# Earlier weight loads, eight tiles split ahead, and older work first in the steps of a feed-forward stage

## The chip, the cores and the metric

The kernel runs on one core of a Trainium2 chip. The metric is the device time of one execution in microseconds (us), as the median of several runs. Five engines work side by side, each through its own instructions in order: TensorE (PE in the profile; its weight loads are PEld), VectorE (DVE), ScalarE (ACT), GpSimd (POOL) and SyncE (SP), which here only issues DMAs. An instruction that waits holds up all that stand behind it on its engine. Matmul results land in PSUM banks; everything else lives in SBUF, whose tiles are reused, so that a load into a tile waits for the last reader of what it held.

## What is computed

Attention in which each query keeps its 32 best keys, then a soft mixture of 8 experts, then a feed-forward layer, over 2304 tokens of width 512:

```python
scores = scale * q @ k.T;  attn = softmax(top 32 of each row);  x = attn @ v
logits = x @ phi                                   # 32 slots, 4 for each expert
slot_in = softmax(logits, axis=0).T @ x
slot_out[e] = relu(slot_in[e] @ w1[e]) @ w2[e]      # 8 experts, 512 -> 1024 -> 512
x = softmax(logits, axis=1) @ slot_out
h = x @ w_in                                       # 512 -> 2048
g = where(h >= 1, h, where(h <= -1, 0, (h + 1)**2 / 4))
out = g @ w_out                                    # 2048 -> 512
```

`w_in` and `w_out` come as 64-bit floats, read by the kernel as pairs of 32-bit integers and rebuilt as float32.

## The kernel before

**Attention** runs first, by a hand-written order over 16 pairs of heads. During it the first weight tiles are loaded, and `w_in` is converted and stored as `cv_d`.

**Weight tiles.** `worder` lists 88 tiles, `w_0` to `w_87`, nearly all of 128 x 1024 words (512 KB): 32 of `w1`, 32 of `w2`, eight of the converted `w_in` (`cv_d`) and 16 of `w_out`. All go through SP's queue in the order of that list. Each needs a free slot, a piece of SBUF that was used before: `wload` takes the next slot of `wfree` and notes it in `ring`, so that `ring` holds the slots in the order in which they were filled, which is also the order in which they are freed. A few slots consist of two halves in different places (`half_slots`); tiles of `w1`, `w2` and `cv_d` fit there by two DMAs of half the size, `w_out` tiles don't. After attention nine slots are taken out of `ring` (`tr_slots`, `w_slots`, `mix_slots`: scratch for rebuilding `w_out`, for its split tiles and for the mixture weights), and all other slots are refilled in turn.

**The expert part.** `ex_in` multiplies the slot inputs by `w1` (tile line L827, rows `h<-w,siT`), for experts 0 to 3 (`g` = 0) and 4 to 7, in four chunks `c`; `ex_out` multiplies by `w2` (L850, rows `so<-w,h1T`) in eight chunks. Between them stand transposes (`ex_turn`, `mix_turn`, `ex_place`) and the mixture weights (`mix_load`, `mix_norm`, `mix_split`).

**The feed-forward part.** Since a token is a mixture of 32 slots, `slot_out @ w_in` is computed once: `m_first` gives the first quarter of its columns as `m4[0]`, `m_rest` the other three in one PSUM tile, `m_split` divides them into a high and a low part, and `m_spread` makes `m4[1]` to `m4[3]` of them. A step `(t, f)` then treats 384 tokens (block `t` of 6) and 128 of the 2048 columns (`f` of 16). `emit_h` computes h in a PSUM tile `h_ps` (two banks, `ps_m`, which `m_ps` tiles share), two ACT passes (L952, L953) and a maximum with a minimum on DVE (L954) give g; g is split into a rounded part and a rest (`ghl`: a copy and a subtraction, L961 or L963, and L964); `emit_o` adds nine matmuls (L975) to the three output tiles. There are 96 steps, numbered here from 0: steps 0 to 31 alternate `t` = 0 and 1 for each `f`, and from 32 on a block is done at a time. h and g of a step are issued three steps ahead (`GA` = 3).

**Rebuilding a tile of `w_out`** (`prep`) takes two ACT passes (L934, L938), two DVE shifts (L935, L936), an addition on GpSimd (L939), one DVE operation (L941), an ACT copy into the rounded part `wh` (L943) and a DVE subtraction for the rest `wl` (L944). Four tiles are done in the expert part, and twelve within the first 26 steps, begun in step `(1, f)` and finished in the next.

Of the kernel before, what the change touches and what calls it, by code (L numbers as in the profile page):

```python
# [73 lines left out]
def kernel_body(tc, qT, kT, vP, phi, w1, w2, w_in, w_out, out, fast, flag):  # L74
# [851 lines left out]
    def prep(f, k):  # L926
        x64 = wtile[(4, 0, f)]
        hf = x64[:, :, 1].bitcast(F32)
        if k == "a":
# [3 lines left out]
        if k == "a":  # L933
            nc.scalar.activation(tf, hf, AF.Abs)  # L934
            nc.vector.tensor_scalar(tf, tf, 2.0 ** -15, None, op0=ALU.max)  # L935
            nc.vector.tensor_scalar(t, t, 3, None, op0=ALU.logical_shift_left)  # L936
        elif k == "r":
            nc.scalar.activation(r.bitcast(F32), x64[:, :, 0].bitcast(U32), AF.Identity, bias=two, scale=2.0 ** -51)  # L938
            nc.gpsimd.tensor_tensor(t, t, r, op=ALU.add)  # L939
        else:  # L940
# [4 lines left out]
            del preps[f]

    def emit_h(s_):
        t, f = s_
# [6 lines left out]
        gs[s_] = g

    def emit_g(s_, on_act=False):
        g = gs.pop(s_)
        gh, gl = (x[:, :BLK] for x in ring_tile("g", g_slots, "ghl", F32R))
        if on_act:  # L960
# [43 lines left out]
    ex_in(0, range(1))
    for f in (0, 1):
        prep(f, "a")
        prep(f, "r")
    ex_in(0, range(1, 4))
    prep(0, "b")
# [117 lines left out]
```

## Time and profile before

| | |
|---|---|
| three runs | 889.18, 889.29 (median), 891.91 us |
| the profiled execution | 890.73 us, span 888.9 us |
| PE, DVE, ACT, POOL busy | 94%, 77%, 73%, 49% of the span |
| mean granted TensorE clock | 0.977 of full speed |
| attention | to about 565 us |
| experts | about 566 to 624 us |
| feed-forward | about 624 us to the end |

The span is the time from the first to the last instruction; the execution's own time holds 1.8 us more around it. Times in the rows are counted from the start of the span.

### The profile page before, as it was taken

The numbers are of one execution on the slowest core, as the hardware profiler recorded it, in microseconds if no ns is written. First come the engines' busy times: TensorE is split into PE (matmuls) and PEld (weight loads), VectorE is DVE, ScalarE is ACT, GpSimd is POOL, SyncE is SP. The second block draws the span as 40 slices with busy tenths as digits, with TensorE's granted clock in tenths as the row PEclk, the third lists the DMA queues.
The fourth block names the chain that finished last, engine by engine and source line by source line (L and its number), as shares of the span: only waits on it lengthen the run. The fifth ranks groups of instructions, "written<-read, shape, count | busy, mean of one in ns | idle before, by whom it ended". The sixth has DMA issues, their size and how long they took to land.

```text
span 888.9 us, 17733 instructions
## 1 busy us (share of the span) xinstructions
PE 837.3 (94%) x5695; PEld 680.8 (77%) x5695; DVE 686.8 (77%) x3113; ACT 645.0 (73%) x1294; POOL 439.6 (49%) x462
## 2 busy tenths in 40 slices
PE   4889999999999999999999998898878789999997
PEld 3679988988998898988888997422356568888885
DVE  6999999989999999999999982360366676666663
ACT  5688999889899888899888895331366666545452
POOL 2788888878788877788877770110011210000000
PEclk9699999999999999999999999799998899999999
DMA  8463564464255244255245416399900001000001
GB/s 239 141 171 93 154 186 117 133 173 120 93 151 127 76 127 119 70 139 139 79 112 140 165 31 243 100 397 403 409 16 1 1 1 72 36 1 37 1 36 39
DMA packets 45046, 108.60 MB, mean 122 GB/s; under 512 B 8240, under 2 KB 8240, under 8 KB 44944
## 3 DMA queue, kind: packets, MB, share of 16 engines
q1 hardware_dynamic: 44624, 106.73, 39.1%
q8 instruction: 47, 0.77, 0.4%
q10 hardware_dynamic: 320, 0.66, 0.3%
q14 instruction: 55, 0.45, 0.1%
HBM read 70.70 MB, written 8.91 MB: 90 GB/s over the span
## 4 chain that ended last, share of the span: by engine, by line
PE 77%; DVE 9%; ACT 6%; DMA 5%; issue 1%; SPq 0%; POOL 0%; ACTq 0%; DVEq 0%; POOLq 0%
PE s_ps L310 20%; PE o_ps L975 17%; PE av_ps L484 14%; PE pt_ps L456 6%; DMA w<-in_moe_w_dram 5%; PE s_ps L412 4%; PE av_ps L485 3%; PE rem_ps L229 3%; PE moe_ps L574 2%; DVE cand L337 2%; PE h_ps L950 2%; DVE rg L954 2%; ACT rg L953 1%; ACT rg L952 1%; PE xT_ps L533 1%
## 5 line engine op out<-in xcount | busy, mean ns | idle before, releaser
L310 PE MATMUL s_ps<-kh,q 128*128 128x288 f32 x640 | 208.7, 343 | 15.2 <-DVE q L265 9.1
L975 PE MATMUL o_ps<-whl,ghl 128*128 128x512 f32 x864 | 219.4, 399 | 1.1 <-DVE mhl L897 1.1
L975 PEld LDWEIGHTS o_ps<-whl,ghl 128*128 128x128 f32 x864 | 164.1, 191 | 35.5 <-issue 1.5
L444 POOL TENSOR_TENSOR ssb<-ssb,pen 128x576 f32<-128x576 f32 x141 | 180.7, 1286 | 18.1 <-ACT pen L441 15.7
L310 PE MATMUL s_ps<-kl,q 128*128 128x288 f32 x640 | 181.8, 300 | 0.0
L337 DVE MAX8 cand<-ssb 128x8 f32<-128x82 f32 (+1 forms) x1008 | 164.3, 228 | 4.6 <-ACT ssb L328 3.8
L310 PEld LDWEIGHTS s_ps<-kh,q 128*128 128x128 f32 x640 | 124.3, 194 | 33.5 <-DVE q L265 9.4
L484 PE MATMUL av_ps<-v_sb,ptb 128*128 128x65 f32 (+1 forms) x1280 | 147.1, 261 | 0.4 <-ACT xT L546 0.4
L484 PEld LDWEIGHTS av_ps<-v_sb,ptb 128*128 128x128 f32 (+1 forms) x1280 | 141.1, 180 | 5.1 <-issue 2.9
L310 PEld LDWEIGHTS s_ps<-kl,q 128*128 128x128 f32 x640 | 125.1, 196 | 0.3
L421 DVE MAX8 l<-s_ps 128x8 f32<-128x576 f32 x144 | 109.2, 758 | 17.7 <-PE s_ps L412 17.3
L441 ACT ACTIVATE pen<-ssb,kb 128x576 bf16<-128x576 f32 x141 | 110.4, 793 | 3.2 <-POOL kb L437 2.1
L447 ACT ACTIVATE ssb<-ssb,nm 128x576 f32<-128x576 f32 x141 | 109.0, 785 | 0.6 <-POOL ssb L444 0.6
L328 ACT COPY ssb<-s_ps 128x576 f32<-128x576 f32 x144 | 91.3, 642 | 24.8 <-PE s_ps L310 20.9
L952 ACT ACTIVATE rg<-h_ps,half 128x384 f32<-128x384 f32 x96 | 55.6, 579 | 70.3 <-PE h_ps L950 70.1
L939 POOL TENSOR_TENSOR tr_l<-tr_l 128x512 int32<-128x512 int32 x16 | 21.2, 1322 | 168.2 <-DVE ghl L964 95.2
L954 DVE SCALAR_TENSOR_TENSOR rg<-h_ps,rg 128x384 f32<-128x384 f32 x96 | 53.5, 557 | 62.8 <-ACT rg L953 62.8
L395 POOL TENSOR_SCALAR mb<-ssb,top 128x576 bf16<-128x576 f32 x48 | 83.4, 1737 | 17.0 <-DVE top L344 6.4
L466 ACT COPY ptb<-pt_ps 128x512 f32<-128x512 f32 x144 | 82.5, 598 | 3.8 <-PE av_ps L484 3.7
L456 PE MATMUL pt_ps<-ident,ssb 128*128 128x128 f32 x576 | 84.3, 273 | 0.3 <-ACT ptb L466 0.2
L397 DVE TENSOR_SCALAR_CACHE_REDUCE mb<-ssb,top 128x576 bf16<-128x576 f32 x96 | 75.8, 802 | 0.0
L344 DVE MAX8 top<-cand 128x8 f32<-128x56 f32 x432 | 73.6, 207 | 0.1
(160 smaller groups left out, 1322.1 us busy)
## 6 DMA issues: line engine op xcount, KB each, us to landing
w<-in_moe_w_dram SPq DMA_DIRECT2D x56, 512.0 KB, 7.0
q<-qst SPq DMA_DIRECT2D x60, 160.0 KB, 3.1
kh<-kst SPq DMA_DIRECT2D x60, 144.0 KB, 2.5
kl<-kst SPq DMA_DIRECT2D x60, 144.0 KB, 2.8
x<-in_moe_w_in_dram SPq DMA_DIRECT2D x16, 512.0 KB, 3.8
w<-in_moe_w_out_dram SPq DMA_DIRECT2D x16, 512.0 KB, 10.2
v_sb<-in_v_dram SPq DMA_DIRECT2D x16, 325.0 KB, 2.9
raw_t<-in_q_dram SPq DMA_DIRECT2D x15, 320.0 KB, 3.7
```

The costliest lines, as they stand in the source:

```text
L310: nc.tensor.matmul(s[:, hf, :HS], a, w, start=(n == 0), stop=(n == len(terms) - 1), skip_group_check=True)
L328: nc.scalar.copy(st[u]["ssb"][:, j], st.pop((u, j))[:, :, :HS])
L337: nc.vector.max(st[u]["cand"][:, j, 8 * g:8 * g + 8], row(u, j)[:, S * g // NSEG:S * (g + 1) // NSEG])
L395: nc.gpsimd.tensor_scalar(st[u]["mb"][:, j], row(u, j), t_u, None, op0=ALU.is_ge)
L421: nc.vector.max(st[u]["l8"][:, j], st.pop((u, j))[:, :, :HS])
L441: nc.scalar.activation(pen, row(u, j), AF.Relu, bias=st[u]["kb"][:, j:j + 1], scale=-BIG)
L444: nc.gpsimd.tensor_tensor(row(u, j), row(u, j), st.pop((u, "pen", j)), op=ALU.subtract)
L447: nc.scalar.activation(row(u, j), row(u, j), AF.Exp, bias=st[u]["nm"][:, j:j + 1], scale=0.125)
L456: nc.tensor.transpose(pt[:, c, :], pr[:, c * P:(c + 1) * P], ident)
L466: nc.scalar.copy(ptb, st.pop((u, "pt", j)))
L484: nc.tensor.matmul(o, pj[:, c, sl], v_sb[:, 4 * jj + c, :], start=(c == 0), stop=False)
L975: nc.tensor.matmul(pos[t][n], a[:, sl], w, start=(f == 0 and k == 0), stop=(f == NF - 1 and k == 2))
```

## The change

1. `worder` has the four first `w_out` tiles four places later, behind four `w2` tiles; the next four `w_out` tiles stand ahead of the last six `cv_d` tiles.
2. The nine slots held back are no longer the first nine of `ring`, but nine whole slots from its ninth place on.
3. `prep` has five parts, 0 to 4. Eight tiles are begun before step 0 (the last two are finished in steps 0 to 3). The other eight follow one in every three steps, from step 3, each spread over four steps.
4. Within a step, what belongs to older data comes first on every engine; in two of three such steps the rounding copy of g is put off to the next step, on ACT.
5. `m_rest` and `m_split` move from ahead of step 0 into step 2, and their PSUM tile into the two banks of `ps_m`; the `e_ps` bank that it had is left to the output tiles.

```diff
+SOON = 8
-    worder[32:32] = [(4, 0, f) for f in range(EARLY)]
-    worder += [(2, 0, n) for n in range(2 * NHP)] + [(4, 0, f) for f in range(EARLY, NF)]
+    worder[36:36] = [(4, 0, f) for f in range(EARLY)]
+    worder += [(2, 0, 0), (2, 0, 1)] + [(4, 0, f) for f in range(EARLY, SOON)]
+    worder += [(2, 0, n) for n in range(2, 2 * NHP)] + [(4, 0, f) for f in range(SOON, NF)]
...
-    tr_slots = [ring.pop(0) for _ in range(3)]
-    w_slots = [ring.pop(0) for _ in range(EARLY)]
-    mix_slots = [ring.pop(0) for _ in range(2)]
+    held = [x for x in ring[8:] if x in slots_a + slots_b[:3] + cv_slots][:5 + EARLY]
+    ring = [x for x in ring if x not in held]
+    tr_slots, mix_slots, w_slots = held[:3], held[3:5], held[5:]
...
-            mx["m"] = ps_f.tile([P, 512], F32, name="m_ps1", tag="e_ps")
+            mx["m"] = ps_m.tile([P, 512], F32, name="m_ps1", tag="m_ps")
...
-    begin = {int((f - EARLY) * 1.1): f for f in range(EARLY, NF)}
+    todo = {}
+    for f in range(SOON - 2, SOON):
+        for k, lag in ((1, 0), (2, 1), (3, 1), (4, 2)):
+            todo.setdefault((f - SOON + 2 + lag, k), []).append(f)
+    for f in range(SOON, NF):
+        for k, lag in enumerate((0, 1, 2, 2, 3)):
+            todo.setdefault((3 + 3 * (f - SOON) + lag, k), []).append(f)
+    behind = []
     def step(i):
...
+        if i == 2:
+            m_rest(1)
+            m_rest(2)
+            m_rest(3)
+            mhl.extend(m_split())
+        if i % 8 == 4 and i // 8 < NC1 - 1:
+            m_spread(i // 8 + 1, *mhl)
         if nxt:
             emit_h(nxt)
-        if new is not None:
-            prep(new, "a")
+        work(4, 2, 1)
+        late_g = behind.pop() if behind else None
+        if late_g:
+            emit_c(late_g, nc.scalar)
+        work(3, 0)
         if nxt:
-            emit_g(nxt, new is not None)
-        if new is not None:
-            prep(new, "r")
-        if t == 0 and f - 1 in begin:
-            prep(begin[f - 1], "b")
+            emit_m(nxt)
+        if late_g:
+            emit_d(late_g)
+        if nxt:
+            if any((j, 0) in todo for j in (i, i - 1)):
+                behind.append(nxt)
+            else:
+                emit_c(nxt, nc.vector)
+                emit_d(nxt)
         emit_o(t, f, range(NS))
...
     m_first()
-    m_rest(1)
-    for s_ in steps[:2]:
-        emit_h(s_)
-        emit_g(s_)
-    m_rest(2)
-    m_rest(3)
-    for s_ in steps[2:GA]:
-        emit_h(s_)
-        emit_g(s_)
-    mhl = m_split()
+    prep(5, 0)
+    emit_h(steps[0])
+    for k in (2, 3):
+        prep(4, k)
+    emit_h(steps[1])
+    prep(5, 1)
+    emit_g(steps[0])
+    prep(4, 4)
+    emit_g(steps[1])
+    prep(6, 0)
+    for k in (2, 3):
+        prep(5, k)
+    emit_h(steps[2])
+    prep(5, 4)
+    emit_g(steps[2])
+    prep(7, 0)
```

Here `emit_m` is the maximum and minimum, `emit_c` the rounding copy and `emit_d` the subtraction of g; `work(k, ...)` issues the parts of `prep` that `todo` names for the step.

**SP's queue at the end of attention.** `w_28` to `w_31` are the last tiles of `w1`; `w_32` and those after it stand behind them. Before:

```order
L165 DMA w_27_9084<-in_moe_w1_dram 128x1024
L165 DMA w_26_9080<-in_moe_w1_dram 128x1024
L165 DMA w_28_9086<-in_moe_w1_dram 128x1024
L165 DMA w_29_9132<-in_moe_w1_dram 128x1024
L165 DMA w_30_9191<-in_moe_w1_dram 128x1024
L165 DMA w_31_9216<-in_moe_w1_dram 128x1024
L165 DMA w_32_9415<-in_moe2_w_out_dram 128x1024
L165 DMA w_33_9417<-in_moe2_w_out_dram 128x1024
L165 DMA w_34_9419<-in_moe2_w_out_dram 128x1024
L165 DMA w_35_9421<-in_moe2_w_out_dram 128x1024
L165 DMA w_36_9423<-in_moe_w2_dram 128x512
L165 DMA w_36_9424<-in_moe_w2_dram 128x512
```

After:

```order
L167 DMA w_33_9294<-in_moe_w2_dram 128x512
L167 DMA w_28_9086<-in_moe_w1_dram 128x1024
L167 DMA w_29_9132<-in_moe_w1_dram 128x1024
L167 DMA w_33_9295<-in_moe_w2_dram 128x512
L167 DMA w_30_9191<-in_moe_w1_dram 128x1024
L167 DMA w_31_9216<-in_moe_w1_dram 128x1024
L167 DMA w_34_9298<-in_moe_w2_dram 128x512
L167 DMA w_34_9299<-in_moe_w2_dram 128x512
L167 DMA w_35_9302<-in_moe_w2_dram 128x512
L167 DMA w_35_9303<-in_moe_w2_dram 128x512
L167 DMA w_36_9431<-in_moe2_w_out_dram 128x1024
L167 DMA w_37_9433<-in_moe2_w_out_dram 128x1024
```

The first four `w2` tiles, as eight halves, have moved ahead of the `w_out` tiles and among the last loads of attention. Behind the third of the `w_out` tiles the next load goes into the slot of `w_2` (freed by the first chunk of `ex_in`) where it went into the slot of `w_11` (third chunk).

**PE from `m_first` to the first steps.** Rows with `m_ps_9850` or `m_ps_9856` are `m_first`, the rows with 32x512 are `m_rest`, `h_ps` is h of a step and `o_ps` its output. Before:

```order
L880 MATMUL m_ps_9850<-w_9503,so_9543 128x512 x2
L880 MATMUL m_ps_9850<-w_9505,so_9543 128x512 x2
L889 MATMUL m_ps_9857<-w_9507,so_9543 32x512 x2
L889 MATMUL m_ps_9857<-w_9509,so_9543 32x512 x2
L950 MATMUL h_ps<-cT_9599,m_0_9402 128x384 x2
L889 MATMUL m_ps_9857<-w_9511,so_9543 32x512 x2
L889 MATMUL m_ps_9857<-w_9513,so_9543 32x512 x2
L889 MATMUL m_ps_9857<-w_9515,so_9543 32x512 x2
L889 MATMUL m_ps_9857<-w_9517,so_9543 32x512 x2
L950 MATMUL h_ps<-cT_9599,m_0_9402 128x384 x2
L975 MATMUL o_ps_0_9915<-whl,ghl 128x512 x3
```

After:

```order
L883 MATMUL m_ps_9856<-w_9505,so_9543 128x512 x2
L955 MATMUL h_ps<-cT_9601,m_0_9418 128x384 x4
L991 MATMUL o_ps_0_9926<-whl,ghl 128x512 x3
L991 MATMUL o_ps_1_9927<-whl,ghl 128x512 x3
L991 MATMUL o_ps_2_9928<-whl,ghl 128x512 x3
L955 MATMUL h_ps<-cT_9601,m_0_9418 128x384
L991 MATMUL o_ps_0_9955<-whl,ghl 128x512 x3
L991 MATMUL o_ps_1_9956<-whl,ghl 128x512 x3
L991 MATMUL o_ps_2_9957<-whl,ghl 128x512 x3
L892 MATMUL m_ps_9967<-w_9515,so_9543 32x512 x2
L892 MATMUL m_ps_9967<-w_9517,so_9543 32x512 x2
```

All twelve rows of `m_rest` (six in this print, of which two are shown) have moved behind the matmuls of steps 0 and 1, and h of the fourth step stands ahead of step 0 in both.

**ACT and DVE in the steps, around the rebuilding of one `w_out` tile (`w_81`).** `tr_l` and `whl` are the tile's, `rg` and `ghl` a step's. ACT before, two steps:

```order
L952 ACTIVATE rg_10178<-h_ps_10176,half_77 128x384
L953 ACTIVATE rg_10178<-rg_10178 128x384
L934 ACTIVATE tr_l_10183<-w_81_9529 128x512
L961 CAST ghl_10187<-rg_10179 128x384
L938 ACTIVATE tr_l_10183<-w_81_9529,two_95 128x512
L952 ACTIVATE rg_10204<-h_ps_10202,half_77 128x384
L953 ACTIVATE rg_10204<-rg_10204 128x384
L943 CAST whl_10214<-tr_l_10183 128x512
```

ACT after, three steps:

```order
L957 ACTIVATE rg_10081<-h_ps_10079,half_77 128x384
L958 ACTIVATE rg_10081<-rg_10081 128x384
L937 ACTIVATE tr_l_10086<-w_81_9529 128x512
L938 ACTIVATE tr_l_10086<-w_81_9529,two_95 128x512
L957 ACTIVATE rg_10103<-h_ps_10101,half_77 128x384
L958 ACTIVATE rg_10103<-rg_10103 128x384
L969 CAST ghl_10090<-rg_10082 128x384
L957 ACTIVATE rg_10124<-h_ps_10122,half_77 128x384
L958 ACTIVATE rg_10124<-rg_10124 128x384
L969 CAST ghl_10111<-rg_10103 128x384
L947 CAST whl_10128<-tr_l_10086 128x512
```

DVE before, from the maximum of the second of these steps:

```order
L954 SCALAR_TENSOR_TENSOR rg_10205<-h_ps_10202,rg_10204 128x384
L963 CAST ghl_10209<-rg_10205 128x384
L964 TENSOR_TENSOR ghl_10210<-rg_10205,ghl_10209 128x384
L941 SCALAR_TENSOR_TENSOR tr_l_10183<-w_81_9529,tr_l_10183 128x512
L944 TENSOR_TENSOR whl_10214<-tr_l_10183,whl_10214 128x512
```

DVE after, from the third of these steps on:

```order
L975 TENSOR_TENSOR ghl_10091<-rg_10082,ghl_10090 128x384
L944 SCALAR_TENSOR_TENSOR tr_l_10086<-w_81_9529,tr_l_10086 128x512
L963 SCALAR_TENSOR_TENSOR rg_10124<-h_ps_10122,rg_10124 128x384
L975 TENSOR_TENSOR ghl_10111<-rg_10103,ghl_10111 128x384
L971 CAST ghl_10132<-rg_10124 128x384
L975 TENSOR_TENSOR ghl_10132<-rg_10124,ghl_10132 128x384
L949 TENSOR_TENSOR whl_10128<-tr_l_10086,whl_10128 128x512
```

On DVE the operation that ACT's copy into `whl` waits for (L941, now L944) stood behind three operations of the newest step and stands ahead of them now; on ACT a tile's first two passes are no longer parted by a copy that waits for DVE, and the tile's three ACT operations are spread over three steps.

## Rows read from the trace of the kernel before

**Rows 1.** The page, part 4: the chain that ended last, shares of the span by engine
```profile
PE 77%; DVE 9%; ACT 6%; DMA 5%; issue 1%; SPq 0%; POOL 0%; ACTq 0%; DVEq 0%; POOLq 0%
```

**Rows 2.** Windows: busy us of PE, PEld, DVE, ACT, POOL; granted clock, DMA share, GB/s
```profile
550.00:565.00 15.00, 12.63 (x126) 9.78 (x124) 4.76 (x22) 5.92 (x26) 0.00 (x0) 0.89 0.02 7
565.00:577.00 12.00, 11.04 (x80) 3.20 (x72) 4.35 (x8) 4.90 (x9) 2.86 (x2) 0.72 0.49 159
577.00:645.00 68.00, 62.10 (x299) 20.89 (x299) 24.44 (x50) 20.81 (x42) 2.84 (x2) 1.00 1.03 403
651.30:732.07 80.77, 65.89 (x256) 49.77 (x256) 54.74 (x107) 52.74 (x98) 14.19 (x11) 0.92 0.00 1
732.07:874.48 142.41, 142.41 (x632) 117.52 (x631) 94.17 (x192) 77.13 (x141) 0.00 (x0) 1.00 0.08 28
```

**Rows 3.** Waits of SP's queue, 480 to 700: total us, times, longest
```profile
SPq L165 <- PE moe_ps L622: 17.3, 1, 17.3
SPq L165 <- PE h L827: 7.9, 3, 7.4
```

**Rows 4.** Timeline of SP, 560 to 640: start, us, what
```profile
565.27 9.64 SPq L165 DMA_DIRECT2D w<-in_moe_w_out_dram  x4
```

**Rows 5.** Timeline of PE: start, us, what, idle before and its releaser
```profile
566.53 9.67 PE L827 MATMUL h<-w,siT 128*32 128x512 f32 x64 [0.36 <-ACT siT L735]
...
620.57 1.90 PE L850 MATMUL so<-w,h1T 128*32 128x512 f32 x10 [0.31 <-DMA w<-in_moe_w_dram]
...
628.20 3.62 PE L889 MATMUL m_ps<-w,so 128*32 128x512 f32 x8
...
638.05 2.24 PE L975 MATMUL o_ps<-whl,ghl 128*128 128x512 f32 x9
...
651.30 2.26 PE L975 MATMUL o_ps<-whl,ghl 128*128 128x512 f32 x9
```

**Rows 6.** Groups of instructions, 651 to 732: busy us, mean ns, idle before and releaser
```profile
L952 ACT ACTIVATE rg<-h_ps,half 128x384 f32<-128x384 f32 x26 | 14.9, 573 | 0.1
L954 DVE SCALAR_TENSOR_TENSOR rg<-h_ps,rg 128x384 f32<-128x384 f32 x25 | 13.9, 557 | 15.8 <-ACT rg L953 15.8
L953 ACT ACTIVATE rg<-rg 128x384 f32<-128x384 f32 x26 | 13.6, 525 | 0.8
L950 PE MATMUL h_ps<-cT,m 128*128 128x384 f32 x26 | 11.1, 426 | 12.2 <-DVE rg L954 11.9 <-ACT m L906 0.3
L938 ACT ACTIVATE tr_l<-w,two 128x512 f32<-128x512 uint32 x11 | 8.4, 766 | 0.0
L934 ACT ACTIVATE tr_l<-w 128x512 f32<-128x512 f32 x11 | 7.2, 652 | 0.0
L943 ACT CAST whl<-tr_l 128x512 fp32r<-128x512 f32 x11 | 6.8, 620 | 25.5 <-DVE tr_l L941 25.5
L935 DVE TENSOR_SCALAR tr_l<-tr_l 128x512 f32<-128x512 f32 x11 | 4.7, 427 | 0.0
L905 PE MATMUL m_ps<-mhl,twice 32*128 32x512 f32 x4 | 1.5, 442 | 2.9 <-DVE rg L954 2.9
```

**Rows 7.** Timeline of VectorE and GpSimd
```profile
572.03 1.29 POOL L939 TENSOR_TENSOR tr_l<-tr_l 128x512 int32<-128x512 int32 x1 [33.99 <-DVE tr_l L936]
...
572.64 0.97 DVE L935 TENSOR_SCALAR tr_l<-tr_l 128x512 f32<-128x512 f32 x1 [0.78 <-ACT tr_l L934]
...
628.92 0.69 DVE L883 TENSOR_TENSOR m<-m_ps,m 64x512 fp32r<-64x512 f32 x1 [4.41 <-ACT m L882]
```

**Rows 8.** Windows of lowered clock, columns as in the stages
```profile
565.00:571.50 6.50, 5.54 (x33) 1.37 (x29) 1.04 (x4) 1.49 (x3) 0.00 (x0) 0.50 0.71 226
674.50:681.00 6.50, 5.05 (x12) 4.10 (x13) 3.97 (x8) 4.10 (x9) 1.18 (x1) 0.50 0.00 0
```

**Rows 9.** Timeline of PE in the second of these windows
```profile
675.95 0.69 PE L950 MATMUL h_ps<-cT,m 128*128 128x384 f32 x1 [2.10 <-DVE rg L954]
676.43 4.04 PE L975 MATMUL o_ps<-whl,ghl 128*128 128x512 f32 x9
```

More of the change, by code (lines that the diff above doesn't have):

```diff
@@ L748, in kernel_body @@
     ps_f = tail.enter_context(tc.tile_pool(name="ps_f", bufs=3, space=PSUM))
-    wfree.extend([whole(wB, f"wB{n}", 1) for n in range(NB)])
+    wb_slots = [whole(wB, f"wB{n}", 1) for n in range(NB)]
+    wfree.extend(wb_slots)
     wload(NB)
-    tr_slots = [ring.pop(0) for _ in range(3)]
-    w_slots = [ring.pop(0) for _ in range(EARLY)]
-    mix_slots = [ring.pop(0) for _ in range(2)]
+    held = [x for x in ring[8:] if x in slots_a + slots_b[:3] + cv_slots][:5 + EARLY]
+    ring = [x for x in ring if x not in held]
+    tr_slots, mix_slots, w_slots = held[:3], held[3:5], held[5:]
     while wnext[0] < len(worder):
@@ L953, in emit_h, with emit_m, emit_c @@
         nc.scalar.activation(r, r, AF.Square)
+        gs[s_] = ph, r, g
+    def emit_m(s_):
+        ph, r, g = gs[s_]
         nc.vector.scalar_tensor_tensor(g, ph, 1.0, r, op0=ALU.max, op1=ALU.min)
[L955 to L960, printed above, removed]
+        gs[s_] = g, [x[:, :BLK] for x in ring_tile("g", g_slots, "ghl", F32R)]
+    def emit_c(s_, on):
+        g, (gh, gl) = gs[s_]
+        if on is nc.scalar:
             nc.scalar.copy(gh, g)
@@ L963, in emit_g, with emit_d @@
             nc.vector.tensor_copy(gh, g)
+    def emit_d(s_):
+        g, (gh, gl) = gs[s_]
         nc.vector.tensor_tensor(gl, g, gh.bitcast(F32), op=ALU.subtract)
-        gs[s_] = (gh, gl)
+        gs[s_] = gh, gl
+    def emit_g(s_):
+        emit_m(s_)
+        emit_c(s_, nc.vector)
+        emit_d(s_)
     def emit_o(t, f, rows):
@@ L986, in step, with work @@
         nxt = steps[i + GA] if i + GA < len(steps) else None
-        new = begin.get(f) if t == 1 else None
-        if t == 1 and f % 4 == 1 and f // 4 < NC1 - 1:
-            m_spread(f // 4 + 1, *mhl)
+        def work(*ks):
+            for k in ks:
+                for x in todo.get((i, k), ()):
+                    prep(x, k)
+        if i == 2:
[5 more added lines that the diff above has]
+            m_spread(i // 8 + 1, *mhl)
         if nxt:
             emit_h(nxt)
-        if new is not None:
-            prep(new, "a")
-        if nxt:
-            emit_g(nxt, new is not None)
-        if new is not None:
-            prep(new, "r")
-        if t == 0 and f - 1 in begin:
-            prep(begin[f - 1], "b")
+        work(4, 2, 1)
[3 more added lines that the diff above has]
+        work(3, 0)
+        if nxt:
+            emit_m(nxt)
[7 more added lines that the diff above has]
+                emit_d(nxt)
         emit_o(t, f, range(NS))
+    mhl = []
     nc.vector.tensor_scalar_add(run_s, run_s, 1e-9)
     nc.vector.reciprocal(run_s, run_s)
[L1004 to L1009, printed above, removed]
+    ex_in(0, range(4))
     ex_relu(0)
+    ex_in(1, range(2))
     mix_load()
-    ex_in(1, range(2))
     ex_turn(0)
     nc.scalar.activation(mx["lt"], mx["lt"], AF.Exp)
-    prep(1, "b")
+    prep(0, 0)
     mix_norm()
-    prep(2, "a")
-    prep(2, "r")
+    prep(0, 1)
     ex_in(1, range(2, 4))
     ex_relu(1)
+    prep(1, 0)
+    prep(1, 1)
     tell()
@@ L1023, in kernel_body @@
     mix_split(0)
-    prep(3, "a")
-    prep(3, "r")
-    prep(2, "b")
+    for k in (2, 3, 4):
+        prep(0, k)
     ex_turn(1)
     mix_split(1)
+    prep(2, 0)
+    prep(2, 1)
     ex_out(0, range(4, 6))
@@ L1031, in kernel_body @@
     mix_split(2)
-    prep(3, "b")
+    for k in (2, 3, 4):
+        prep(1, k)
+    prep(3, 0)
+    prep(3, 1)
     ex_out(0, range(6, 8))
@@ L1036, in kernel_body @@
     mix_split(3)
+    for f in (2, 3):
+        for k in (2, 3, 4):
+            prep(f, k)
     ex_out(1, range(2))
@@ L1044, in kernel_body @@
     ex_place(1)
+    prep(4, 0)
+    prep(4, 1)
     m_first()
-    m_rest(1)
-    for s_ in steps[:2]:
-        emit_h(s_)
-        emit_g(s_)
-    m_rest(2)
-    m_rest(3)
-    for s_ in steps[2:GA]:
-        emit_h(s_)
-        emit_g(s_)
-    mhl = m_split()
+    prep(5, 0)
[14 more added lines that the diff above has]
+    prep(7, 0)
     for i in range(len(steps) - NLAST):
```

18 lines of the change are left out of this document (10 added, 8 removed).

## Prediction

> **What bounds the kernel now.** The chain of work that ended last is the first view: 77% of the span lies on PE [rows 1], so what counts is where PE waits. The windows by stage say where [rows 2]. From 732.07 on PE is busy throughout at full clock: 63 steps in 142.41 us, 2.26 us a step. The stage ahead, steps 4 to 28, takes 80.77 us for 25 steps, 3.23 each, with every engine partly idle. From 577 to 645 the DMA engines are full (share 1.03, 403 GB/s), and from 550 to 565 they are idle (0.02). So there are three places: weight loads that start late, the opening of the feed-forward part, and steps 4 to 28. All before and behind stays as it is.
>
> *Loads.* SP's waits name the reason [rows 3]: 17.3 us for the end of attention, behind which the first `w_out` tile stands, then 7.4 us for `ex_in`, since the slot behind the three free ones is that of the third chunk. Four loads take from 565.27 to 574.91 to be issued [rows 4]; `ex_in` frees its slots from 566.53 to 576.2 [rows 5]. In the stream that follows PE waits for the last `w2` tile until 620.57 [rows 5]. I call this moment E.
>
> *Steps 4 to 28.* By groups, PE's h matmul waits 12.2 us, nearly all for the maximum on DVE (a bank comes free with it), and ACT's copy into `whl` waits 25.5 us over 11 tiles for DVE [rows 6]: ACT stands still for 2.3 us per tile behind an operation that DVE does last, and the h work of the newest step is queued behind that copy. Twenty-five steps at 2.26 are 56.5 us, two spreads (steps 11 and 19) 1.5 [rows 6]: 22.8 us are lost, 2.07 per tile, falls of the clock included.
>
> **A. The loads: E 10 us earlier.** A tile takes 512 KB / 403 GB/s = 1.30 us [rows 2]. Four `w2` tiles move to where the DMA engines idle, and need not pass in the full stretch. Behind the three `w_out` tiles that start at 565.3 in both, the queue goes on with slots that a quarter of `ex_in` frees (566.53 + 9.67/4 = 569, a little later as the clock is low then), where it now goes on at 574.9. Some 5 us of idle DMA are filled, four tiles. Eight tiles fewer stand ahead of the last `w2` tile at 577: 8 x 1.30 = 10.4. I take off 0.4, as three or four loads can't hide the time from issue to first data. Bounds: 13 us (no idle at all) and 0 (below). What could take it back: the last four `w2` tiles load into slots from which `prep` of tiles 0 to 3 must have read; laid out in the new order, tile 3's read on DVE comes about 602, and its slot is wanted about 606 (both estimates), so some 4 us of cover; and PE must have worked off the earlier `ex_out` rows; 62.1 us busy of 68 [rows 2] with waits counted out leaves it some room. New E: 610.6.
>
> **B. The opening: 7 us longer.** Now step 0 starts 17.5 us behind E and step 4 30.7 (638.05, 651.30) [rows 5]. `m_first` ends at E+7.7 in both. Then `m_rest` fills PE until E+17.5 (628.20 to 638.05, some 9 us without the h matmuls) while h of the first steps is made. After the change nothing covers it: `m4[0]` is ready at E+9.0 (628.92+0.69 now [rows 7]); h 0.43; ACT first does tile 5's passes (0.65+0.77, to E+9.6), then the two passes of h (0.57+0.53), DVE the maximum (0.56): E+11.3 [rows 6]. PE's queue holds h of step 3 ahead of step 0, and that needs a bank, free with the maximum of step 1; between these DVE does step 0's split and `wl` of tile 4 (some 2.2): E+14 for step 0. h of step 4 needs the maximum of step 2, on ACT behind tile 6's passes and tile 5's copy: E+17.5, step 1 ends at E+20.3. `m_rest` follows, 9 us, to E+29.3; step 2 to E+31.8; step 3 waits for `m_split` (two copies and two subtractions in turn, 0.6 to 0.7 each) and ends at E+34.5; the spread, and h of step 7 behind DVE's arrears: step 4 at E+36.3. I add 1.4 for the low clock and for DVE beside GpSimd (both below): E+37.7 against E+30.7. Bounds: +3 (no arrears) and +11.
>
> **C. Steps 4 to 28: 21.2 us shorter.** Eight tiles are left, one per three steps. ACT's and DVE's work per step is read from the steady stretch: 94.17/63 = 1.49 us on DVE, 77.13/63 = 1.22 on ACT; the stage gives per tile (54.74 - 25 x 1.49)/11 = 1.6 on DVE and (52.74 - 25 x 1.22)/11 = 2.0 on ACT [rows 2]. In three steps that is 4.5+1.6 = 6.1 on DVE and 3.7+2.0 on ACT, there with one more copy of g that leaves DVE (0.5, like a pass of its size): 6.2. PE takes 6.78. No engine is over, and DVE has done L941's successor before ACT asks. Laid out in order, the maximum ends 2.2 to 2.8 us after its h; h two steps on needs the bank 4.5 us after. So PE goes at 2.26, but for two spreads (0.75 and about 0.55 of waiting each) and 0.5 spare: 56.5+2.6+0.5 = 59.6 against 80.8. Bounds: 57 and 75 (rivals).
>
> **D.** From step 29 to the end nothing changes. Bits that cost nothing: eight half loads instead of four later ones (same bytes, DMA idle), and `m_ps1` in another bank, whose waits are in B.
>
> **Sum.** -10.0+7.0-21.2 = -24.2 us, or 888.9-24.2 = 864.7 of span. The profiled execution took 890.73, 1.4 above the median of the runs; on the median, 889.3-24.2 = **865**.
>
> **GpSimd beside DVE.** One row shows a cost that the change meets more often: a DVE shift that began at 572.64 took 0.97 us, with a GpSimd addition running from 572.03 to 573.32; elsewhere it takes 0.43 [rows 6, 7]. In the loop before, DVE mostly stood idle while GpSimd added; afterwards it is nearly full. The Trainium skill, "SBUF — State Buffer", section "SBUF: two separate sides", says that the two engines' common port pair is an exclusive lock, held for a whole instruction; the row agrees. By the row alone the delay is what was left of the 1.29 us addition; by the page it falls on copies, shifts and two-input operations, so that it could strike twice per tile, which would make the third stage some 15 us longer than I sum (an estimate). The order puts a maximum (one input from PSUM) beside most additions, which is why I count 0.5.
>
> **The rivals.**
> 1. *DVE becomes the bound of the third stage.* It has 6.78-6.1 = 0.7 us to spare in three steps, and decides once it loses more: with two additions' length, 2.6, lost per tile PE loses 1.9, 8 x 1.9 = 15; half of that makes **872**. For: the 0.97 us row. Against: the layout above.
> 2. *The loads win nothing*, because a slot is late (tile 3's read is over 4 us later than I place it) or PE can't keep up: E stays, **875**. Against: PE waits for DMA at E and nothing else [rows 5].
> 3. *Tiles go on stalling PE as they do*: 8 x 2.07 = 16.6 in place of the 1.1 that I count behind the spreads' own matmuls, **880**. For: ACT's load, 6.2 of 6.78, is tight. Against: the copy that waited finds its input done.
> 4. *Slower: the clock stays low.* PE idles from E+7.7 to E+14 but for three h matmuls, longer than anywhere from 577 on. After idle stretches the granted clock was 0.50 from 565.0 to 571.5, and from 674.5 to 681.0 [rows 8], the 1.2 of its two levels 1.2 and 2.4 GHz; nine output matmuls then took 4.04 us, not 2.26 [rows 5, 9], 1.8 per step. Such a fall in the opening costs little, as step 1 waits anyway. If the clock stayed low beyond 24.2/1.8 = 13 steps, the kernel would be slower; through all 29 steps, +52: **917**. The page "TensorE: Matmul & The Clock Gate" of the Trainium skill, section "What's actually happening", says that the low clock is the default and that activity releases it; by that rule the gap does bring a fall and the full steps behind it end it. Rows 8 agree with both: 6.5 us each, and it rose once PE had work in a row.
>
> **How the numbers follow.** Chances: the forecast, 857 to 869, 0.60; rival 1, 0.17; rival 2, 0.12; rival 3, 0.07; rival 4, 0.04. The range must leave out no more than 0.2: below, loads and opening at their better bounds (-3, -4) with a little kept, 857; above, it takes in rivals 1 and 2, 876. 0.3% of 889 is 2.7 us, about what a measurement of this kernel can tell from no change. Only rival 4 can end slower: 0.04; a mixture of rivals 2 and 3 with a bad opening ends within 0.3% (0.01); faster 0.95.
>
> **What would show it.** Right: DMAs running between 550 and 565; the last `ex_out` matmuls at 610 to 611; a gap on PE of 5 to 7 us behind `m_first` with a low clock for some 6 us; `m_rest` behind step 1; then steps 2.3 us apart from the fifth on, ACT's copy into `whl` without its wait, the steady stretch reached near 708. Wrong: E later than 613; a DVE busy share near 1 with doubled shifts and copies in steps 4 to 28; steps over 2.5 us; a clock of 0.50 lasting over 10 us.

## The result, and the profile after

The changed kernel takes 863.53 us (median of 4 runs, 862.73 to 867.28), the kernel before 889.55 on the same chip (4 runs, 889.18 to 891.91): a ratio of 0.971, 95% interval 0.9677 to 0.9743. The profiled execution took 863.71 us with a span of 861.9, 27.0 less than before. The forecast was 865, with 24.2 less of span.

The page's part 4, the chain that ended last, answers to [rows 1]: PE's share went from 77% to 85%, and ACT's from 6% to 1%.

```profile
PE 85%; DVE 7%; DMA 5%; ACT 1%; issue 1%; POOL 0%; ACTq 0%; DVEq 0%; SPq 0%; POOLq 0%
```

The windows by stage answer to [rows 2], with the same columns. From 550 to 565 the DMA engines now move 84 GB/s (7 before), and from 565 to 577 271 (159 before). In the fourth row, steps 4 to 28, PE is busy in all of the 58.30 us at full clock, where it had 65.89 of 80.77. The fifth is the steady stretch.

```profile
550.00:565.00 15.00, 12.64 (x122) 9.81 (x125) 4.61 (x21) 6.00 (x26) 0.00 (x0) 0.89 0.25 84
565.00:577.00 12.00, 11.04 (x89) 2.96 (x85) 0.69 (x2) 1.43 (x3) 0.00 (x0) 0.72 0.82 271
577.00:645.00 68.00, 54.71 (x315) 23.91 (x307) 40.64 (x76) 32.04 (x61) 10.37 (x8) 0.90 0.90 354
646.83:705.13 58.30, 58.30 (x255) 47.06 (x255) 44.93 (x91) 47.39 (x91) 10.38 (x8) 1.00 0.00 1
705.13:847.50 142.37, 142.37 (x631) 117.46 (x631) 92.84 (x190) 77.14 (x141) 0.00 (x0) 1.00 0.08 28
```

PE's timeline answers to [rows 5]: a wait of 3.40 us ahead of the last `ex_out` rows, these rows, the last transposes, `m_first`, step 0, `m_rest`, and the steps 4, 11, 12 (a spread lies between these two) and 29.

```profile
605.45 0.37 PE L816 MATMUL c_ps<-ident,c 64*128 64x64 f32 x1 [3.40 <-ACT cT L818]
605.75 3.64 PE L853 MATMUL so<-w,h1T 128*32 128x512 f32 x16
...
610.22 4.04 PE L853 MATMUL so<-w,h1T 128*32 128x512 f32 x32
614.99 0.66 PE L865 MATMUL soT_ps<-ident,so_sb 128*128 128x128 f32 x4 [0.73 <-ACT so_sb L860]
616.36 3.70 PE L883 MATMUL m_ps<-w,so 128*128 128x512 f32 x8 [0.71 <-DVE so L869]
...
626.79 3.75 PE L991 MATMUL o_ps<-whl,ghl 128*128 128x512 f32 x9
...
632.73 7.11 PE L892 MATMUL m_ps<-w,so 128*32 128x512 f32 x24
...
646.83 2.26 PE L991 MATMUL o_ps<-whl,ghl 128*128 128x512 f32 x9
...
662.68 2.23 PE L991 MATMUL o_ps<-whl,ghl 128*128 128x512 f32 x9
...
665.78 2.26 PE L991 MATMUL o_ps<-whl,ghl 128*128 128x512 f32 x9
...
705.13 2.23 PE L991 MATMUL o_ps<-whl,ghl 128*128 128x512 f32 x9
```

Four marks on PE account for the difference. The last transposes of the experts start at 614.99; before it was 623.20 (620.57 + 1.90 + 0.73, the same wait for `so_sb`), so 8.2 us are won there. This line is of the kernel before:

```profile
623.20 0.66 PE L862 MATMUL soT_ps<-ident,so_sb 128*128 128x128 f32 x4 [0.73 <-ACT so_sb L857]
```

From this mark to step 4 it takes 31.84 us instead of 28.10: 3.7 are lost. Steps 4 to 28 take 58.30 instead of 80.77: 22.5 won. From step 29 to the end it is 156.8 in both. -8.2 + 3.7 - 22.5 = -27.0.

The groups of steps 4 to 28 answer to [rows 6]: PE's h waited 12.2 us, now 0.7; ACT's copy into `whl` waited 25.5 us for DVE, now not at all; GpSimd's eight additions are there too.

```profile
L963 DVE SCALAR_TENSOR_TENSOR rg<-h_ps,rg 128x384 f32<-128x384 f32 x25 | 13.9, 556 | 12.3 <-ACT rg L958 12.3
L942 POOL TENSOR_TENSOR tr_l<-tr_l 128x512 int32<-128x512 int32 x8 | 10.4, 1297 | 50.8 <-ACT rg L957 28.5 <-DVE tr_l L941 22.3
L955 PE MATMUL h_ps<-cT,m 128*128 128x384 f32 x26 | 9.1, 348 | 0.7 <-DVE rg L963 0.7
L947 ACT CAST whl<-tr_l 128x512 fp32r<-128x512 f32 x8 | 4.9, 615 | 0.0
```

From 577 to step 29 the clock fell twice, to the lower of its two levels, as windows in the columns of [rows 8] show: behind PE's wait from 602.1 to 605.5, and in the opening, where PE had run nothing but h matmuls since 620.06.

```profile
603.00:609.50 6.50, 4.05 (x18) 0.95 (x19) 2.48 (x7) 1.31 (x3) 0.00 (x0) 0.50 1.04 400
623.50:630.00 6.50, 4.38 (x10) 3.31 (x11) 5.33 (x10) 4.39 (x9) 0.87 (x1) 0.50 1.03 410
```

### The profile page after: what moved, and what is told of

It is laid out like the page before. It is cut to its first block, busy times and chain, and to the rows that moved or that the text cites. A ratio compares the mean times of both kernels' runs of the same rounds, so it can differ in the third digit from the quotient of the medians.

```text
span 861.9 us, 17740 instructions
## 1 busy us (share of the span) xinstructions
PE 817.4 (95%) x5695; PEld 677.2 (79%) x5695; DVE 685.9 (80%) x3109; ACT 645.1 (75%) x1298; POOL 438.6 (51%) x462
## 4 chain that ended last, share of the span: by engine, by line
PE 85%; DVE 7%; DMA 5%; ACT 1%; issue 1%; POOL 0%; ACTq 0%; DVEq 0%; SPq 0%; POOLq 0%
PE o_ps L991 23%; PE s_ps L312 20%; PE av_ps L486 14%; PE pt_ps L458 7%; PE s_ps L414 4%; PE av_ps L487 3%; PE rem_ps L231 3%; DMA w<-cv_d 2%; PE moe_ps L576 2%; PE h_ps L955 2%; DMA w<-in_moe_w_dram 2%; DVE cand L339 2%; PE h L830 2%; PE xT_ps L535 1%; PE rem_ps L233 1%; DVE l L423 1%
## 5 line engine op out<-in xcount | busy, mean ns | idle before, releaser
L991 PE MATMUL o_ps<-whl,ghl 128*128 128x512 f32 x864 | 217.0, 396 | 0.0
```

What stands on the lines that cost most here:

```text
L991: nc.tensor.matmul(pos[t][n], a[:, sl], w, start=(f == 0 and k == 0), stop=(f == NF - 1 and k == 2))
```

## The experiments

All ratios are to the kernel before on the same chip. "The mark" is the start of the last transposes (614.99 in the changed kernel), and "the stretch" is the time from step 4 to step 29. The runs went to three chips, on which the kernel before took 888.99 us (runs 1 to 4), 890.18 (runs 6 and 8 to 10) and 889.42 (runs 5, 7, 11 and 12).

### The loads, and what holds the last `ex_out` rows

**1. The loads alone**, on the kernel before:

```diff
-    worder[32:32] = [(4, 0, f) for f in range(EARLY)]
+    worder[36:36] = [(4, 0, f) for f in range(EARLY)]
...
-    tr_slots = [ring.pop(0) for _ in range(3)]
+    held = [x for x in ring[8:] if x in slots_a + slots_b[:3] + cv_slots][:5 + EARLY]
```

> Only parts 1 and 2 of the change (order of the loads, slots held back), on the kernel before. Theory 'the terms are separate': the start of the last transposes ahead of m_first (623.20 before, 614.99 after) comes 8 to 10 us earlier, steps 4 to 28 keep their 80.8 us, the time is 879 to 881. Rival 'the loads only help since the preparations of tiles were moved too': the old order of the expert part holds PE, under 4 us are won, 885 or more.

883.36 us (882.9 to 884.17), ratio 0.9938 (0.9922 to 0.9955): 5.6 us won, between the two. The mark came at 615.09, 8.1 earlier, as in the changed kernel, and the stretch kept its length (80.65). But the first `m_rest` matmuls waited 1.24 us for a `cv_d` tile, which now stands behind four `w_out` tiles, so that step 4 came only 6.7 earlier (644.57 against 651.30). The first theory's mark was right, its time not. The changed kernel also prepares tiles 0 to 3 later among the experts' matmuls, which the list of its changes leaves out; this run keeps the old order there and reaches the mark at the same time.

**2. The first nine slots held back again:**

```diff
-    held = [x for x in ring[8:] if x in slots_a + slots_b[:3] + cv_slots][:5 + EARLY]
+    tr_slots = [ring.pop(0) for _ in range(3)]
```

> The changed kernel with the first nine slots of ring held back again (part 2 undone). SP then waits again for the third chunk of ex_in and some 5 us of DMA time are idle. Theory 'loads set E': everything from the last ex_out on is 5 us later, 868.5. Rival 'PE sets E, since DVE and ACT hold it up between 594 and 605': the last w2 tile had some us to spare, and less than 2 us are lost, 863.5 to 865.5.

869.22 us (867.98 to 871.98), ratio 0.9786 (0.976 to 0.9812): 5.7 more than the changed kernel, by the first theory. SP's longest wait for `ex_in` is 7.3 us again (3.3 in the changed kernel), and from 565 to 577 the DMA engines move 170 GB/s (271). PE now waits for nearly every one of the last `w2` tiles (two such rows stand here), and the mark is at 619.76.

```profile
615.85 1.05 PE L852 MATMUL so<-w,h1T 128*32 128x512 f32 x2 [0.23 <-DMA w<-in_moe_w_dram]
617.13 1.90 PE L852 MATMUL so<-w,h1T 128*32 128x512 f32 x10 [0.23 <-DMA w<-in_moe_w_dram]
```

**3. The late halves of tiles 2 and 3 behind `mix_turn(2)`:**

```diff
-    for f in (2, 3):
-        for k in (2, 3, 4):
-            prep(f, k)
+    prep(2, 2)
+    prep(3, 2)
     ex_out(1, range(2))
     ex_place(0)
     mix_turn(2)
+    for f in (2, 3):
+        for k in (3, 4):
+            prep(f, k)
```

> The changed kernel with the last two parts of preparation (ACT's copy into whl and DVE's subtraction) of tiles 2 and 3 behind ex_place(0) and mix_turn(2), where both engines stood idle from 606 to 614. Theory 'PE sets E': the wait of 3.4 us at 605.45 goes and with it the low clock of the ex_out matmuls behind it (16 in 3.64 us, elsewhere 1.92); the last transposes start 3 to 4.5 us earlier, near 611, and the time is 859 to 860.5. Rival 'loads set E': the last ex_out matmuls wait for their w2 tiles, under 1 us is won, 862.5 to 863.5.

863.95 us (863.15 to 869.04), ratio 0.9741 (0.9707 to 0.9774): nothing won. The wait of 3.40 us is down to 0.68, and PE, early now, waits for the loads instead, with the last ten matmuls at 611.62:

```profile
602.37 0.35 PE L816 MATMUL c_ps<-ident,c 64*128 64x64 f32 x1 [0.68 <-ACT cT L818]
602.65 3.47 PE L853 MATMUL so<-w,h1T 128*32 128x512 f32 x16
...
611.62 1.90 PE L853 MATMUL so<-w,h1T 128*32 128x512 f32 x10 [0.23 <-DMA w<-in_moe_w_dram]
614.25 0.66 PE L865 MATMUL soT_ps<-ident,so_sb 128*128 128x128 f32 x4 [0.73 <-ACT so_sb L860]
```

So in the changed kernel PE's wait and the low clock behind it cost almost nothing: PE caught up by the time the last tile landed. That the last 32 matmuls ran there without a wait for DMA did not mean that DMA was early; the two were level. The loads set E.

### Steps 4 to 28

**4. The newest step's work first again**, with eight tiles and their spacing as changed:

```diff
+        fresh = nxt and any((i, k) in todo for k in (0, 3))
         if nxt:
             emit_h(nxt)
-        work(4, 2, 1)
...
+        work(0)
+        if nxt:
+            emit_m(nxt)
+            emit_c(nxt, nc.scalar if fresh else nc.vector)
+            emit_d(nxt)
+        work(1, 2, 3, 4)
```

The copy of g is then never put off; `fresh` says in which steps it goes to ACT.

> The changed kernel with the newest step's work first in each step again (h, the next tile's ACT passes, maximum, copy, subtraction, then the other parts of a tile), eight tiles and their spacing as they are. Theory 'the order in the step did it': ACT's copy into whl waits for DVE again, some 1.5 to 2 us per tile are lost, 8 x 1.5 to 2 = 12 to 16, time 875 to 880. Rival 'fewer tiles and their spacing did it': steps stay near 2.3 us, time within 3 us of 863.5.

882.73 us (881.16 to 886.58), ratio 0.9926 (0.9895 to 0.9957): 19 us slower than the changed kernel, the first theory and more. The windows' columns show the stretch: 75.62 us, PE busy in 65.47 of it, a mean clock of 0.91.

```profile
647.88:723.50 75.62, 65.47 (x255) 50.29 (x255) 46.26 (x89) 47.58 (x92) 10.29 (x8) 0.91 0.00 1
```

PE's timeline shows one round of it: h waits for the maximum at a spread, the clock falls, and the step takes 3.42 us.

```profile
669.60 0.73 PE L908 MATMUL m_ps<-mhl,twice 32*128 32x512 f32 x2 [0.18 <-DVE rg L963]
671.99 0.69 PE L955 MATMUL h_ps<-cT,m 128*128 128x384 f32 x1 [1.66 <-DVE rg L963]
672.47 3.42 PE L991 MATMUL o_ps<-whl,ghl 128*128 128x512 f32 x9
```

**5. The new order alone**, on the loads, slots, opening and twelve tiles of before:

```diff
+    for f in range(EARLY, NF):
+        for k, lag in enumerate((0, 1, 2, 2, 3)):
+            todo.setdefault((1 + 2 * int((f - EARLY) * 1.1) + lag, k), []).append(f)
...
-            if any((j, 0) in todo for j in (i, i - 1)):
+            if any((j, 0) in todo for j in (i,)):
```

> The kernel before with the new order in the step alone (older data first, the rounding copy of g put off in one of two steps): loads, held slots and opening as before, twelve tiles in the loop, one begun in 2.2 steps. Theory 'the order in the step did most of the stretch': its steps come near 2.3 us but for the spreads, steps 4 to 28 take 62 to 66 us instead of 80.8, time 870 to 874. Rival 'order and spacing only work together': as with tiles in every two steps, and worse, the spreads collide with tiles, 70 us or more for the stretch, 878 or more.

873.6 us (873.06 to 876.33), ratio 0.9821 (0.98 to 0.9843): the first theory. The run keeps the later preparation of tiles 0 to 3; its mark is at 622.02, 1.2 us ahead of the kernel before, which is no part of the stretch. The stretch takes 65.62 us:

```profile
649.10:714.72 65.62, 60.85 (x256) 47.96 (x256) 52.68 (x107) 51.16 (x97) 14.20 (x11) 0.97 0.00 1
```

**6. One tile in every two steps** instead of three:

```diff
-            todo.setdefault((3 + 3 * (f - SOON) + lag, k), []).append(f)
+            todo.setdefault((3 + 2 * (f - SOON) + lag, k), []).append(f)
```

> The changed kernel with one tile begun in every two steps instead of three, the order in the step as it is (the copy of g is put off in one of two steps). Theory 'capacity': DVE then has 2 x 1.49 + 1.6 = 4.58 us of work for two steps of 4.52 on PE, so that PE loses at most 0.1 per tile and nothing in sum; 863 to 866. Rival 'the spacing did most of what steps 4 to 28 gained': h waits for the maximum again, 1 us or more per tile, 871 or more.

869.86 us (869.33 to 870.34), ratio 0.9762 (0.9718 to 0.9806): between the theories, and both miss the place. Away from the spreads PE keeps its 2.27 us per step; all that is lost (64.46 us for the stretch, 6.2 more) is lost at the two spreads. In the changed kernel step 11 to step 12 takes 3.10 us with the spread between them (662.68, 665.78); here 5.58, and a step at low clock follows:

```profile
662.04 2.21 PE L991 MATMUL o_ps<-whl,ghl 128*128 128x512 f32 x9
664.80 0.73 PE L908 MATMUL m_ps<-mhl,twice 32*128 32x512 f32 x2 [0.55 <-DVE rg L963]
667.34 0.44 PE L955 MATMUL h_ps<-cT,m 128*128 128x384 f32 x1 [1.80 <-DVE rg L963]
667.62 3.81 PE L991 MATMUL o_ps<-whl,ghl 128*128 128x512 f32 x9
```

By the code, the spread's PSUM tile takes one of the two `ps_m` banks, so that there the next h has to wait for a maximum at once, and ACT has one more copy. That this is the cause is argued, not shown: no run took the spread's bank away.

**7. The copy of g never put off, always on DVE:**

```diff
-            if any((j, 0) in todo for j in (i, i - 1)):
-                behind.append(nxt)
-            else:
-                emit_c(nxt, nc.vector)
-                emit_d(nxt)
+            emit_c(nxt, nc.vector)
+            emit_d(nxt)
```

> The changed kernel with the rounding copy of g always at once and on DVE. By the sum of work in the stretch DVE goes from 44.9 us busy to 44.9 + 16 x 0.36 = 50.7 of 58.3, ACT from 47.4 to 39.4. Theory 'there is room on DVE': 862.5 to 865. Rival 'DVE was near its bound, and only the copies on ACT kept it under': the maximum comes late, PE loses 0.7 us or more per tile, 869 or more.

866.16 us (864.65 to 866.49), ratio 0.9729 (0.9709 to 0.9748): between the two again. By the medians that is 2.6 us slower, no more than a measurement can tell; the stretch decides. It takes 60.22 us, 1.9 more, and these are again lost at the two spreads (4.13 and 3.99 from step to step). DVE is busy 55.74 us, not 50.7: the timelines of VectorE and GpSimd show why.

```profile
655.88 1.29 POOL L942 TENSOR_TENSOR tr_l<-tr_l 128x512 int32<-128x512 int32 x1 [6.10 <-DVE tr_l L941]
...
655.62 0.55 DVE L963 SCALAR_TENSOR_TENSOR rg<-h_ps,rg 128x384 f32<-128x384 f32 x1
656.27 1.11 DVE L971 CAST ghl<-rg 128x384 fp32r<-128x384 f32 x1
...
659.15 0.36 DVE L971 CAST ghl<-rg 128x384 fp32r<-128x384 f32 x1
```

A copy that starts while the addition runs (655.88 to 657.17) takes 1.11 us and ends 0.2 behind it; the next one takes 0.36. The maximum beside the same addition takes its usual 0.55. In the stretch of the changed kernel the ten copies left on DVE take 0.36 us each: putting the others off to ACT keeps the copies away from the additions.

The four kernels of the stretch side by side:

| order in the step | tiles begun | stretch, us | of it at the spreads | elsewhere (21 steps) |
|---|---|---|---|---|
| newest first | 12, one in 2.2 steps (before) | 80.77 | 22.40 | 58.37 |
| newest first | 8, one in 3 (run 4) | 75.62 | 19.81 | 55.81 |
| older first | 12, one in 2.2 (run 5) | 65.62 | 16.85 | 48.77 |
| older first | 8, one in 3 (changed) | 58.30 | 10.78 | 47.52 |

The order, with the copies of g put off as part of it, is worth 15 to 17 us, fewer tiles and wider spacing 5 to 7. The fourth column is the time of four steps: the two with a spread behind them, and the one after each. Away from the spreads the order alone comes within 1.3 us of the changed kernel; at the spreads it takes the wider spacing too.

### The opening

**8. `m_rest` and `m_split` ahead of step 0 again**, the rest as changed:

```diff
     m_first()
+    m_rest(1)
     prep(5, 0)
...
     emit_g(steps[1])
+    m_rest(2)
+    m_rest(3)
...
     emit_g(steps[2])
+    mhl.extend(m_split())
```

> The changed kernel with part 5 undone: m_rest and m_split ahead of step 0 again, their PSUM tile in the e_ps bank, eight tiles and the order in the steps as changed. Theory 'the opening costs what PE idles and what the low clock takes behind m_first': m_rest(1) waits about 1.3 us for a cv_d tile (as in the run with the loads alone), the rest fills PE while h is made; step 4 starts near 644.5 where the changed kernel has 646.83, time 860.5 to 862. Rival 'the work on tiles 4 to 6 holds h whatever PE does': nothing won, 863 to 865.

864.97 us (863.94 to 869.02), ratio 0.9702 (0.9657 to 0.9747): nothing won. The profiled execution was the longest of the four, 869.02 us; it reached the mark 3 us later than the changed kernel's. From the mark to step 5 it takes 35.96 us (618.04, 654.00), in the changed kernel 34.11 (614.99, 649.10). In this execution three things eat what the filled gap gives: a wait for a `cv_d` tile, pieces of `m_rest` that are slower than the whole, and waits for the maximum (0.98 and 1.47) with a low clock at the first spread.

```profile
624.37 3.62 PE L892 MATMUL m_ps<-w,so 128*32 128x512 f32 x8 [1.27 <-DMA w<-cv_d]
...
628.47 5.37 PE L892 MATMUL m_ps<-w,so 128*32 128x512 f32 x16
...
647.85 0.73 PE L908 MATMUL m_ps<-mhl,twice 32*128 32x512 f32 x2 [0.98 <-DVE rg L963]
650.04 0.69 PE L955 MATMUL h_ps<-cT,m 128*128 128x384 f32 x1 [1.47 <-DVE rg L963]
650.53 3.46 PE L991 MATMUL o_ps<-whl,ghl 128*128 128x512 f32 x9
```

**9. The same with tile 4's and 5's early parts ahead of `m_first`**, where ACT and DVE stood idle, with run 3's edit, and with h of step 2 between the last two thirds of `m_rest`:

```diff
+    prep(5, 0)
+    prep(4, 2)
+    prep(4, 3)
     m_first()
+    m_rest(1)
...
```

> As the run with m_rest ahead of step 0, and with tile 4's parts 2 and 3 and tile 5's ACT passes ahead of m_first, where ACT and DVE stood idle, and the late halves of tiles 2 and 3 behind mix_turn(2). Theory 'DVE and ACT delay h by what stands ahead of it': h of step 0 comes 1.4 us earlier, step 4 at 643 to 644, time 859.5 to 861. Rival 'the cv_d tiles decide once m_rest stands ahead of step 0': the same as with m_rest ahead alone.

866.88 us (864.86 to 868.09), ratio 0.9728 (0.968 to 0.9775): by the rival, no better than run 8. `m_rest` again waits 1.26 us for `cv_d`, and in three pieces takes 3 x 3.62 us.

**10. The same with all `cv_d` tiles ahead of the fifth `w_out` tile**, and with the work on tiles 4 and 5 behind h of steps 0 and 1:

```diff
-    worder += [(2, 0, 0), (2, 0, 1)] + [(4, 0, f) for f in range(EARLY, SOON)]
-    worder += [(2, 0, n) for n in range(2, 2 * NHP)] + [(4, 0, f) for f in range(SOON, NF)]
+    worder += [(2, 0, n) for n in range(2 * NHP)] + [(4, 0, f) for f in range(EARLY, NF)]
...
```

> As the one before, but with all eight cv_d tiles ahead of the fifth w_out tile in the load order, as before the change, and tile 4's passes behind h of steps 0 and 1. Theory 'the cv_d tiles decide': m_rest follows m_first without a wait and PE does not idle there, step 0 near 628 to 629, step 4 near 640 to 642, time 857 to 859. Rival 'the later w_out tiles hold DVE and ACT in the first steps': step 4 no earlier than in the other two, 860 or more.

867.92 us (864.21 to 871.01), ratio 0.9743 (0.9686 to 0.98): the rival. `m_rest` follows `m_first` without a wait, but step 0 starts at 631.78, as the three pieces still take 10.9 us at a granted clock of 1.00, and then h waits 3.32 us for a maximum behind the later tiles' work.

**11. `m_rest` with the quarters in turn**, one edit:

```diff
-        for c in range(NHP):
-            nc.tensor.matmul(mx["m"][32 * n:32 * n + 32], ...
+        for c in range(NHP):
+            for n in range(1, 4):
+                nc.tensor.matmul(mx["m"][32 * n:32 * n + 32], ...
```

> The changed kernel with one edit: in m_rest the loop over the three quarters is the inner one, so that matmuls on different column groups of TensorE follow each other, as in ex_out. Theory 'matmuls on different column groups overlap': ex_out with four groups in turn takes 113 to 120 ns for each of its records (32 in 3.64 us), m_rest one group after another 296 ns (24 in 7.11 us); in turn it takes 3.6 to 4 us. PE's work behind it (steps 2 and 3) comes 3 us earlier, and of this 2 to 3 us arrive at the end, 860.5 to 861.5. Rival 'h of the next steps is held by DVE and ACT, not by PE': m_rest is shorter, but step 4 starts where it did, 863 to 864.

861.04 us (859.06 to 867.4), ratio 0.9685 (0.9656 to 0.9714): the first theory. The 24 matmuls take 3.63 us instead of 7.11, and step 4 comes 29.21 us behind the mark (612.93, 642.14) instead of 31.84, 2.6 less.

```profile
631.16 3.63 PE L892 MATMUL m_ps<-w,so 128*32 128x512 f32 x24
634.73 0.45 PE L955 MATMUL h_ps<-cT,m 128*128 128x384 f32 x1
```

**12. That, with the maxima of steps 0 and 1 ahead of the tiles' work**, and with run 3's edit:

```diff
+    prep(5, 0)
+    prep(4, 2)
     m_first()
...
+    emit_m(steps[0])
+    emit_c(steps[0], nc.vector)
+    emit_m(steps[1])
+    emit_d(steps[0])
...
```

> As the one before, and with tile 5's ACT passes and tile 4's part 2 ahead of m_first, the maxima of steps 0 and 1 ahead of the rest of tiles 4 and 5 on DVE, and the late halves of tiles 2 and 3 behind mix_turn(2). Theory 'what stands ahead of the maxima on ACT and DVE sets step 0': step 0 starts near 625 instead of 626.79, and 1 to 2 us more arrive at the end, 858.5 to 860.5. Rival 'the work only moves behind step 0 and holds the later steps': as the one before or slower.

861.21 us (860.08 to 861.86), ratio 0.9675 (0.9656 to 0.9694): the rival. Step 0 came 1.8 us earlier against the mark (10.05 behind it, not 11.80), and `m_rest` then waited 2.40 us for a bank that a maximum has to free; step 4 came 29.47 behind the mark, as in run 11.

By their medians runs 11 and 12 are the fastest, 2.5 and 2.3 us under the changed kernel. That is less than the 2.7 us that a measurement can tell; the intervals overlap, and it is the distance from the mark to step 4 that shows the gain.

## Why the prediction was right

The three terms miss by 1.8, 3.3 and 1.3 us, the first to the other side, so that 27.0 us stand against 24.2. The mechanisms held; that the sum came as close as it did is in part luck.

**A, the loads: 8.2 us won, 10 predicted.** The mechanism holds (runs 2 and 3: DMA is last). Mis-sized was the term of eight tiles in idle DMA time. By the windows, 1.16 MB more went through from 550 to 565 (77 GB/s x 15 us) and 1.34 MB from 565 to 577 (112 x 12); from 535 to 550 it was 382 GB/s in place of 316, another 0.99, first before, then after:

```profile
535.00:550.00 15.00, 13.41 (x117) 11.24 (x114) 3.03 (x8) 8.63 (x22) 1.15 (x1) 1.00 0.90 316
535.00:550.00 15.00, 13.41 (x116) 11.23 (x117) 3.04 (x8) 8.62 (x22) 1.15 (x1) 1.00 1.00 382
```

At 0.524 MB that is 6.7 tiles, and 6.7 x 1.30 = 8.7 us: four moved to before 565, as counted, but 2.6 in place of four from 565 to 577. SP's queue still waits for `ex_in`, now seven times, 9.2 us together, where it waited three times for 7.9 us [rows 3]:

```profile
SPq L167 <- PE h L830: 9.2, 7, 3.3
```

Rival 2 had a point that the prediction counted against: PE was nearly too late, with 3.40 us of waiting in the middle of the rows. Run 3 shows that it cost nothing here.

**B, the opening: 3.7 us lost, 7 predicted.** Counted from E (612.36, that is the mark less 0.73 and 1.90), step 0 is at E+14.4 and step 1 ends at E+20.4, predicted E+14 and E+20.3. Mis-sized was `m_rest`: 9 us were taken from before, where it ran in pieces of 3.62 and 5.37; in one piece it takes 7.11. The 1.4 for low clock and GpSimd was not needed either: the low clock came (step 0 took 3.75 us), and three copies of g beside GpSimd's additions took 0.88, 1.16 and 1.15 us, but nothing behind them was later than laid out without it. Runs 8 to 10 show that moving `m_rest` behind step 1 cost nothing against leaving it ahead, once tiles 4 to 7 are in the opening. In run 1, without parts 3 to 5 of the change, it takes 29.48 us from the mark to step 4, in the changed kernel 31.84; so 2.4 of the 3.7 came with those parts.

**C, steps 4 to 28: 22.5 us won, 21.2 predicted.** 25 steps of 2.26 are 56.5; the two spreads cost 0.84 and 0.87, not 1.3 each. DVE and ACT had more room than was counted: 44.93 and 47.39 us for 25 steps are 5.4 and 5.7 for three, where the prediction had 6.1 and 6.2; it gave the copy of g to ACT without taking it from DVE. Run 4 shows that the order in the step is the main cause and run 5 that it acts without the rest. One link of the argument is weaker than it was put: the copy into `whl` that waits for DVE. The waits of run 4 and of run 5 (total, times, longest) have the same sum, while run 5 has a stretch 10 us shorter with more tiles:

```profile
ACT whl L947 <- DVE tr_l L944: 11.7, 8, 1.5
```

```profile
ACT whl L945 <- DVE tr_l L942: 11.7, 10, 1.3
```

So that wait alone does not make the loss; what goes with the loss is whether the maximum of the newest step is late for the next h: PE's h waited for it 11.9 us in the kernel before, 8.3 in run 4, 4.6 in run 5 and 0.7 in the changed kernel. Which of the moved operations does this was not separated.

**The rivals.** Rival 1 (DVE the bound through GpSimd) did not come: DVE was busy 44.93 of 58.30 us, and the subtraction beside an addition took 0.70 us, not 0.56. Run 7 shows that it would have, in part, with copies in that place. The Trainium skill, "SBUF — State Buffer", section "SBUF: two separate sides", names as striking against GpSimd the DVE operations with two SBUF inputs or in a two-port mode; run 7's rows agree for the copy (1.11 us for 0.36) and leave the maximum, which reads PSUM, alone. Rival 3 (tiles stall PE as before) is what run 4 looks like. Rival 4 (the clock stays low) did not come: 6.5 us at 0.50 in the opening, and full clock once steps followed each other.

## What to carry to other kernels

Where several engines serve one pipeline, put the work on older data first on each of them, and look at the moments where a bank is short by themselves: run 6 lost only at two spreads, and no run here tried to clear them. Before removing a wait on the bounding engine, find what would be last without it; 3.4 us of idle PE were worth nothing as the loads were level with it. Take the cost of moved work from how it will run (in one piece, in turn), not from how it ran before.
